# Conditioning vectors summed on VectorE, and three vectors broadcast through DRAM, in an adaLN + linear-attention + SwiGLU block

## The chip, the cores and the metric

The kernel runs on one core of a Trainium2 chip. Engines: PE (matmul), PEld (its weight load), DVE (VectorE), ACT (ScalarE), POOL (GpSimd), SP (the engine whose queue issues every DMA here). The metric is device time in microseconds (us), median of several executions. "Span" is first to last instruction; it is about 2 us less than the time. Each execution also reports the mean granted clock of PE: 1.000 is full speed.

## The reference, cut

```python
mod = silu(c) @ w_mod                  # [1,1024] @ [1024, 6*1024]
sa, ca, ga, sb, cb, gb = split(mod)    # six vectors of 1024
h = layernorm(x) * (1 + ca) + sa       # x: 2048 x 1024
x = x + ga * linear_attention(h)       # q, k -> phi = elu+1;  kv = sum k v;  z = sum k
h = layernorm(x) * (1 + cb) + sb
x = x + gb * ((silu(h @ w_gate) * (h @ w_up)) @ w_down)
```

All inputs are bf16. `ga` and `gb` multiply along the free dimension, so every partition needs the whole row ("broadcast"). `sb` and `1+cb` multiply along partitions, so one column per 128 features is enough. `z` is needed in both forms: as columns for the denominators, as a row for the matrix G.

## The kernel before

PE works through: chunk 0 (rows 0 to 511: Q, then K), chunks 1 to 3 (16 groups of eight 128x128x512 matmuls, 8 K and 8 Q), 16 G groups (16 matmuls each), the `wo` stage (16 row tiles), then four chunks of gate/up and down. The kernel's own helper finds the dependencies between engines from the tiles and hands PSUM banks over whole (a reader on another engine holds the bank). The late vectors ga, sb, cb and gb were made thus:

```python
def mod_col_mm(piece, kt):            # 8 per piece, 4 pieces: 256 matmuls of one column
    for m in range(NDT):
        P.pe("matmul", out=PS[:, 6, c0+m:c0+m+1], lhsT=STG[:, kt, m*128:(m+1)*128],
             rhs=SILUC[:, kt:kt+1], ...)
def mod_bcast(dst):                   # row form: columns repeated 128 times, times identity
    for nh in range(2):
        for d4 in range(4):
            P.pe("matmul", out=PS[:, bank, d4*128:(d4+1)*128], lhsT=MODREP[:, 4*nh+d4, :], rhs=IDENT[:], ...)
        P.act("activation", out=dst[:, nh*512:(nh+1)*512], in_=PS[:, bank, :], func=ACT.Copy)
# ... cut: chunks
def phi_evac(bank, dst):              # behind each Q or K group
    P.act(Exp  -> E1);  P.act(Relu -> RL)                 # shortened
    P.dve(min(E1,1)+1e-6 -> E1);  P.dve(RL + E1 -> dst)   # shortened
def th_mod(ch, dt):                   # scale and shift of the transposed h, chunks 2 and 3, all on ACT
    P.act("activation", out=HT[:, buf, dt, :], in_=HT[:, buf, dt, :], func=ACT.Identity, scale=..., bias=...)
# ... cut: after chunk 3
P.dma("wo", WO[:], wov)
# z: column copy, hi/lo split, ZSEL, then ZREP (columns repeated), all on DVE
z_bcast()                             # 16 PE matmuls ZREP x identity, two ACT copies -> ZB
g_group(0); g_evac(0); den()          # den: denominators, reciprocal, DRAM round trip -> RB
for g in range(1, 16):
    g_group(g); g_evac(g)             # 4 PSUM banks
    if g == 2: mod_bcast(GB_B)
```

Of the kernel before, what the change touches and what calls it, by code (L numbers as in the profile page):

```python
# [264 lines left out]
def bass_adaLN_cond__linear_attn_block__swiglu_ffn__prompt_kernel(  # L265
# [22 lines left out]
    with ExitStack() as es:  # L288
# [55 lines left out]
        RL = T("rl", 187 * KB, [128, 3, 512], BF16)  # L344
        MODREP = T("modrep", 190 * KB, [128, NDT, 128], BF16)
        GTMP = T("gtmp", 184 * KB, [128, 2, 512], FP32)
        KVT = T("kvt", 188 * KB, [128, NHG, 128], BF16)
        ZSEL = T("zsel", 193 * KB, [128, 288], BF16)
        ZREP = T("zrep", 194 * KB, [128, 2, NHG, 128], BF16)
        ZB = T("zb", 198 * KB, [128, D], FP32)  # L350
# [19 lines left out]
        RDR = nc.dram_tensor("recip_den", [32, S], BF16).ap()  # L370
        PSB = PS.bitcast(BF16)

        xv = A_x[0].rearrange("(t p) d -> p t d", p=128)
# [46 lines left out]
        P.act("activation", out=SILUC[:], in_=PSB[:, 1, 0:NDT], func=ACT.Silu)  # L420
        P.act("activation", out=ACTWARM[:], in_=SILUC[:], func=ACT.Exp)

        def ln1_stats_ops(st):
# [53 lines left out]
        def th_mod(ch, dt):  # L477
            buf = ch % 2
            P.act("activation", out=HT[:, buf, dt, :], in_=HT[:, buf, dt, :], func=ACT.Identity,
                  scale=MODCOL[:, 0, dt:dt + 1], bias=MODCOL[:, 1, dt:dt + 1])  # L480

# [77 lines left out]
        def phi_evac(bank, dst):  # L559
            i = phi_ctr[0] % 3  # L560
            phi_ctr[0] += 1
            P.act("activation", out=E1[:, i, :], in_=PS[:, bank, :], func=ACT.Exp)
            P.act("activation", out=RL[:, i, :], in_=PS[:, bank, :], func=ACT.Relu)
            P.dve("tensor_scalar", out=E1[:, i, :], in0=E1[:, i, :], scalar1=1.0, scalar2=1e-6,
                  op0=ALU.min, op1=ALU.add)
            P.dve("tensor_tensor", out=dst, in0=RL[:, i, :], in1=E1[:, i, :], op=ALU.add)
# [30 lines left out]

        def mod_col_mm(piece, kt):
            c0 = 8 * piece
            for m in range(NDT):  # L600
                P.pe("matmul", out=PS[:, 6, c0 + m:c0 + m + 1], lhsT=STG[:, kt, m * 128:(m + 1) * 128],
                     rhs=SILUC[:, kt:kt + 1], start=mcol_first[0], stop=(kt == NDT - 1), skip_group_check=True)
                mcol_first[0] = False

# [5 lines left out]

        def mod_col_fin(piece, idx, plus_one, bcast):
            c0 = 8 * piece
            P.dve("tensor_copy", out=MODTMP[:, 0:8], in_=PS[:, 6, c0:c0 + 8])
            if plus_one:
                P.dve("tensor_scalar", out=MODTMP[:, 0:8], in0=MODTMP[:, 0:8], scalar1=1.0, scalar2=None,
                      op0=ALU.add)
            if not bcast:
                P.dve("tensor_copy", out=MODCOL[:, idx, :], in_=MODTMP[:, 0:8])
            else:
                P.dve("tensor_copy", out=MODREP[:], in_=MODTMP[:, 0:8].unsqueeze(2).to_broadcast([128, NDT, 128]))  # L620

        def mod_bcast(dst):
            for nh in range(2):
                bank = [0, 7][nh]
                for d4 in range(4):
                    P.pe("matmul", out=PS[:, bank, d4 * 128:(d4 + 1) * 128], lhsT=MODREP[:, 4 * nh + d4, :],
                         rhs=IDENT[:], start=True, stop=True)
                P.act("activation", out=dst[:, nh * 512:(nh + 1) * 512], in_=PS[:, bank, :], func=ACT.Copy)

        def stg_load(piece):  # L630
            P.dma("stg%d" % piece, STG[:], wmv[:, :, 2048 + 1024 * piece:3072 + 1024 * piece])

# [61 lines left out]

        def piece_mm(side, piece, g0):
            for kt in range(NDT):
                add(side, g0 + kt, lambda kt=kt: mod_col_mm(piece, kt))

        s1, s2, s3 = {}, {}, {}
# [18 lines left out]
        for i, f in enumerate(ops):  # L718
            add(s1, 8 + (i * 7) // 12, f)
        piece_mm(s1, 0, 0)  # L720
        add(s1, 8, lambda: mod_col_fin(0, None, False, True))
        add(s1, 8, lambda: stg_load(1))
        add(s1, 13, lambda: mod_bcast(GA_B))
        add(s1, 15, lambda: ln1_rstd(3))
# [3 lines left out]
        for dt in range(NDT):  # L728
            add(s2, 7 + dt, lambda dt=dt: th_mod(3, dt))
        piece_mm(s2, 1, 0)  # L730
        add(s2, 8, lambda: mod_col_fin(1, 3, False, False))
        add(s2, 8, lambda: stg_load(2))
        piece_mm(s3, 2, 0)
        add(s3, 8, lambda: mod_col_fin(2, 2, True, False))
        add(s3, 8, lambda: stg_load(3))
        for kt in range(NDT):
            add(s3, 14 + kt // 4, lambda kt=kt: mod_col_mm(3, kt))
        chunk(1, s1)
        chunk(2, s2)
        chunk(3, s3)  # L740

        P.dma("wo", WO[:], wov)
        P.dve("tensor_copy", out=ZCOL[:], in_=PS[:, 6, 32:40])
        P.dve("tensor_copy", out=ZHL[:, 0, :], in_=ZCOL[:])
# [3 lines left out]
              in1=MASK4[:].unsqueeze(1).to_broadcast([128, NHG, 4]), op=ALU.mult)  # L748
        for i in range(2):
            P.dve("tensor_copy", out=ZREP[:, i, :, :], in_=ZHL[:, i, :].unsqueeze(2).to_broadcast([128, NHG, 128]))  # L750
        mod_col_fin(3, None, False, True)

        G_BANKS = [2, 3, 4, 5]

        def g_group(g):
            h, dt = g // NDT, g % NDT
            bank = G_BANKS[g % 4]
            for st in range(NST):
                P.pe("matmul", out=PS[:, bank, :], lhsT=XRES[:, st, dt * 128:(dt + 1) * 128],
                     rhs=PKH[h][:, st, :], start=(st == 0), stop=(st == NST - 1))  # L760

        def g_evac(g):
            h, dt = g // NDT, g % NDT
            bank = G_BANKS[g % 4]
            i = g % 2
            P.act("activation", out=GTMP[:, i, :], in_=ZB[:, h * 512:(h + 1) * 512], func=ACT.Copy,
                  scale=MODCOL[:, 1, dt:dt + 1])
            P.dve("scalar_tensor_tensor", out=G[:, dt, h * 512:(h + 1) * 512], in0=PS[:, bank, :],
                  scalar=MODCOL[:, 0, dt:dt + 1], in1=GTMP[:, i, :], op0=ALU.mult, op1=ALU.add)

        def z_bcast():
            for h in range(2):
                for hl in range(4):
                    for i in range(2):
                        P.pe("matmul", out=PS[:, h, hl * 128:(hl + 1) * 128], lhsT=ZREP[:, i, 4 * h + hl, :],
                             rhs=IDENT[:], start=(hl == 0 and i == 0), stop=(i == 1), skip_group_check=True)
                P.act("activation", out=ZB[:, h * 512:(h + 1) * 512], in_=PS[:, h, :], func=ACT.Copy)

        def den():
# [10 lines left out]
            P.wait_for("sp", wr)  # L790
            for hh in range(4):
                src = RDR.rearrange("(g x) s -> x g s", x=4)[hh].unsqueeze(0).to_broadcast([32, NHG, S])
                P.dma("rb%d" % hh, RB[32 * hh:32 * hh + 32, :, :], src)

# [31 lines left out]

        WO_BANKS = [0, 1, 2, 3]

# [11 lines left out]

        z_bcast()
        g_group(0)
        g_evac(0)
        den()
        for g in range(1, 16):
            g_group(g)
            g_evac(g)
            if g == 2:
                mod_bcast(GB_B)
            if 3 <= g <= 6:  # L850
                fold_ga(2 * g - 6)
                fold_ga(2 * g - 5)
            if g == 9:
                kvt_mm(0)
            if 11 <= g <= 14:
                m_mm(g - 11, [0, 1, 7])
            if 8 <= g <= 15:
                scale_pq(g - 8)
        for st in range(4):
# [4 lines left out]
        wo_part(1, 0, range(4))  # L864
        m_mm(4, [4, 5, 7])
        m_mm(5, [4, 5, 7])
        wo_part(1, 1, range(4))
        m_mm(6, [4, 5, 7])
# [40 lines left out]
        for st in range(NST):  # L909
# [3 lines left out]
            if st >= 1:  # L913
                ln2_sq(st - 1)
            if st == 6:
                for jj in range(4):
                    ln2_xn(jj)
# [4 lines left out]
        ln2_sq(NST - 1)  # L922

        y_ctr = [0]
        out_ops = []
        for ch in range(NCH):
            nxt = ch + 1 if ch + 1 < NCH else None
            for ft in range(NFT):
                q = 14 * ch + ft // 2
                slot = q % 4  # L930
                ftl = ft % 2
                gbank, ubank = (ft % 2) * 2, (ft % 2) * 2 + 1
                for dt in range(NDT):
# [9 lines left out]
                if ch == 0 and ft % 2 == 0 and ft < 14:  # L943
                    i = ft // 2
                    wt = WD_A[:, 4 * i:4 * i + 4, :] if i < 4 else WD_B[:, 4 * i - 16:4 * i - 12, :]
                    P.dma("wd%d" % i, wt, wdv[:, 4 * i:4 * i + 4, :])
                if nxt is not None and 4 <= ft < 8:
                    ln2_xn(4 * nxt + (ft - 4))
# [60 lines left out]
```

## Time and profile before

| | before |
|---|---|
| time, first three executions | 860.86 us median (860.63 to 862.51) |
| span of the profiled execution | 856.0 us |
| PE busy | 834.7 us (98%) |
| DVE, ACT busy | 257.8 us (30%), 219.9 us (26%) |

The page's first lines, and its row of the granted clock in 40 equal slices (9 means 90% or more):

```profile
span 856.0 us, 10690 instructions
...
PE 834.7 (98%) x4461; PEld 390.3 (46%) x4461; DVE 257.8 (30%) x563; ACT 219.9 (26%) x375; POOL 35.3 (4%) x50
...
PEclk9999999999999999999999999999999999999999
```

PE, busy for 98% of the span, is the limit. So a change helps if it removes PE work, or if it removes PE idle time. The view of PE's waits lists the idle time by what ended it (total us, times, longest):

```profile
PE ps L178 <- DMA wmsc<-in_w_mod_dram: 8.9, 3, 7.9
PE ps L178 <- ACT ht L178: 2.8, 4, 1.8
PE ps L178 <- DVE zrep L178: 2.5, 2, 2.1
PE ps L178 <- DVE xres L178: 1.9, 4, 1.0
PE ps L178 <- ACT mw L178: 0.5, 2, 0.3
```

The first line is the initial weight load, which the change does not touch. The line for ht holds the border between chunks 1 and 2, the line for zrep the border between chunk 3 and G. PE's timeline around these two borders (start, us, what, and in brackets the idle time in front and its releaser):

```profile
84.91 1.67 PE L178 MATMUL ps<-wqk,ht 128*128 128x512 bf16 x7
88.39 0.39 PE L178 MATMUL ps<-wqk,ht 128*128 128x512 bf16 x1 [1.81 <-ACT ht L178]
88.62 0.34 PE L178 MATMUL ps<-siluc,stg 128*128 128x1 bf16 x8
...
147.74 0.94 PE L178 MATMUL ps<-siluc,stg 128*128 128x1 bf16 x32
150.79 0.23 PE L178 MATMUL ps<-ident,zrep 128*128 128x128 bf16 x1 [2.11 <-DVE zrep L178]
151.40 1.01 PE L178 MATMUL ps<-ident,zrep 128*128 128x128 bf16 x15 [0.37 <-DVE zrep L178]
152.24 3.62 PE L178 MATMUL ps<-pk_85,xres 128*128 128x512 bf16 x16
```

At 88.39 PE waits 1.81 us for the last scaled ht tile; the last of the eight matmuls of chunk 2's first group needs it. Eight one-column matmuls on stg, as at 88.62, take 0.20 us up to the next start. Between the stg matmuls of 147.74 and the first G matmul at 152.24 lie 0.8 us for those matmuls, 2.5 us of idle time in two parts and the 16 zrep matmuls. ACT's timeline shows why ht is late at the first border (start, us, ..., how many):

```profile
84.16 1.53 ACT L178 ACTIVATE ht<-ht,modcol 128x512 bf16<-128x512 bf16 x2
85.57 1.10 ACT L178 ACTIVATE ga_b<-ps 128x512 bf16<-128x512 f32 x2
86.52 0.63 ACT L178 ACTIVATE e_90<-ps 128x512 bf16<-128x512 f32 x1
...
87.48 0.86 ACT L178 ACTIVATE ht<-ht,modcol 128x512 bf16<-128x512 bf16 x1
```

ACT has no gap here: ht scalings, the two copies of the broadcast ga (1.10 us), Exp and Relu follow each other, and the ht tile of 87.48 is the one PE waits for.

### The profile page before, as it was taken

The numbers are of one execution on the slowest core, as the hardware profiler recorded it, in microseconds if no ns is written. First come the engines' busy times: TensorE is split into PE (matmuls) and PEld (weight loads), VectorE is DVE, ScalarE is ACT, GpSimd is POOL, SyncE is SP. The second block draws the span as 40 slices with busy tenths as digits, with TensorE's granted clock in tenths as the row PEclk, the third lists the DMA queues.
The fourth block names the chain that finished last, engine by engine and source line by source line (L and its number), as shares of the span: only waits on it lengthen the run. The fifth ranks groups of instructions, "written<-read, shape, count | busy, mean of one in ns | idle before, by whom it ended". The sixth has DMA issues, their size and how long they took to land.

```text
span 856.0 us, 10690 instructions
## 1 busy us (share of the span) xinstructions
PE 834.7 (98%) x4461; PEld 390.3 (46%) x4461; DVE 257.8 (30%) x563; ACT 219.9 (26%) x375; POOL 35.3 (4%) x50
## 2 busy tenths in 40 slices
PE   4989999999999999999999999999999999999998
PEld 3444444444444444444444444444444444444444
DVE  4667443537554221211122111122111112112111
ACT  4667775212334111110111111011111101111101
POOL 1000000000021000020000003000000200000000
PEclk9999999999999999999999999999999999999999
DMA  9925313461456896560155554025555303553000
GB/s 305 376 107 148 93 57 105 149 148 36 160 124 172 255 306 176 148 154 25 36 159 157 156 150 111 25 62 148 152 159 159 90 25 105 148 148 99 0 25 25
DMA packets 169616, 110.93 MB, mean 130 GB/s; under 512 B 28128, under 2 KB 154208, under 8 KB 169568
## 3 DMA queue, kind: packets, MB, share of 16 engines
q1 hardware_dynamic: 169568, 110.25, 45.1%
q8 instruction: 35, 0.57, 0.3%
q14 instruction: 13, 0.11, 0.0%
HBM read 99.62 MB, written 4.33 MB: 121 GB/s over the span
## 4 chain that ended last, share of the span: by engine, by line
PE 93%; ACT 2%; DMA 2%; SPq 1%; DVE 1%; issue 0%; ACTq 0%
PE ps L178 93%; DMA wmsc<-in_w_mod_dram 2%; SPq L178 1%; ACT ht L178 1%; ACT rl L178 1%; ACT e_90 L178 1%; DMA ht<-xres 0%; DVE zrep L178 0%; ACT mw L178 0%; DVE xres L178 0%; ACT ga_b L178 0%; DVE pqt L178 0%; DVE stats L178 0%; DVE pk_85 L178 0%; DVE zhl L178 0%
## 5 line engine op out<-in xcount | busy, mean ns | idle before, releaser
L178 DVE TENSOR_TENSOR at<-sg,ps 128x512 bf16<-128x512 bf16 x112 | 77.1, 688 | 299.9 <-PE ps L178 298.3
L178 ACT ACTIVATE sg<-ps 128x512 bf16<-128x512 f32 x112 | 66.9, 597 | 310.5 <-PE ps L178 310.5
L178 PE MATMUL ps<-wd_a,at 128*128 128x512 bf16 (+2 forms) x528 | 115.9, 373 | 0.0
L178 PE MATMUL ps<-wd_b,at 128*128 128x512 bf16 (+2 forms) x396 | 88.3, 373 | 0.0
L178 PEld LDWEIGHTS ps<-wd_a,at 128*128 128x128 bf16 x528 | 51.1, 98 | 59.8
L178 ACT ACTIVATE att<-ps 128x512 bf16<-128x512 f32 (+1 forms) x32 | 19.0, 594 | 179.7 <-PE ps L178 179.7
L178 DVE TENSOR_TENSOR ut<-att,gb_b 128x512 bf16<-128x512 bf16 (+1 forms) x32 | 14.3, 447 | 165.1 <-ACT att L178 165.1
L178 PE MATMUL ps<-wqk,ht 128*128 128x512 bf16 x256 | 60.3, 379 | 2.5 <-ACT ht L178 2.5
L178 PE MATMUL ps<-ht,wqk 128*128 128x512 bf16 x256 | 59.2, 386 | 0.3 <-ACT ht L178 0.3
L178 PEld LDWEIGHTS ps<-wd_b,at 128*128 128x128 bf16 x396 | 38.3, 98 | 44.7
L178 PE MATMUL ps<-mw,pqt 128*128 128x512 bf16 x256 | 55.9, 379 | 0.0
L178 PE MATMUL ps<-h2t,guu_108 128*128 128x512 bf16 x224 | 52.9, 379 | 0.0
L178 PE MATMUL ps<-h2t,guu_109 128*128 128x512 bf16 x224 | 52.9, 379 | 0.0
L178 PE MATMUL ps<-h2t,gug_106 128*128 128x512 bf16 x224 | 52.9, 379 | 0.0
L178 PE MATMUL ps<-h2t,gug_103 128*128 128x512 bf16 x224 | 52.9, 379 | 0.0
L178 PE MATMUL ps<-h2t,guu_107 128*128 128x512 bf16 x224 | 52.9, 379 | 0.0
L178 PE MATMUL ps<-h2t,gug_104 128*128 128x512 bf16 x224 | 52.9, 379 | 0.0
L178 PE MATMUL ps<-h2t,gug_105 128*128 128x512 bf16 x224 | 52.9, 379 | 0.0
L178 PE MATMUL ps<-h2t,guu_110 128*128 128x512 bf16 x224 | 52.9, 379 | 0.0
L178 ACT ACTIVATE e_90<-ps 128x512 bf16<-128x512 f32 x64 | 38.7, 604 | 34.5 <-PE ps L178 30.7
L178 POOL TENSOR_SCALAR h2t<-h2t,modcol 128x512 bf16<-128x512 bf16 x32 | 25.2, 808 | 393.6 <-DMA h2t<-xn_111 393.6
L178 PEld LDWEIGHTS ps<-mw,pqt 128*128 128x128 bf16 x256 | 25.0, 98 | 29.7
(108 smaller groups left out, 676.0 us busy)
## 6 DMA issues: line engine op xcount, KB each, us to landing
stg<-in_w_mod_dram SPq DMA_DIRECT2D x4, 2048.0 KB, 8.7
gug_103<-in_B_w_gate_dram SPq DMA_DIRECT2D x14, 512.0 KB, 4.2
guu_107<-in_B_w_up_dram SPq DMA_DIRECT2D x14, 512.0 KB, 5.4
gug_104<-in_B_w_gate_dram SPq DMA_DIRECT2D x14, 512.0 KB, 4.0
guu_108<-in_B_w_up_dram SPq DMA_DIRECT2D x14, 512.0 KB, 5.3
gug_105<-in_B_w_gate_dram SPq DMA_DIRECT2D x14, 512.0 KB, 4.0
guu_109<-in_B_w_up_dram SPq DMA_DIRECT2D x14, 512.0 KB, 5.3
gug_106<-in_B_w_gate_dram SPq DMA_DIRECT2D x14, 512.0 KB, 4.0
```

Source lines behind the costliest of these rows:

```text
L178: return getattr(e, method)(**kw)
```

## The change

The intent: take the late vectors off PE. DVE has idle time (30% busy), so it sums `silu(c)[k] * w_mod[k, :]` in fp32 into a 128x1024 accumulator, splits it into high and low bf16 parts, and PE only adds the 128 partitions up (16 one-column matmuls per vector instead of 64). The rows ga, gb and z are written to DRAM and read back with a broadcast access, instead of PE matmuls and ACT copies. G groups start at once behind chunk 3, with five banks, and z and den are worked out behind them. To make room, half of the ht scalings go to DVE and each phi is finished one group later.

```diff
+        def macc(src, kt):                      # kt == 0: tensor_scalar mult (cut)
+                P.dve("scalar_tensor_tensor", out=ACC[:], in0=src[:, kt, :], scalar=SILUF[:, kt:kt + 1], in1=ACC[:],
+                      op0=ALU.mult, op1=ALU.add)
+        def macc_split():
+            P.dve("tensor_copy", out=MHL[:, 0, :], in_=ACC[:])
+            P.dve("tensor_tensor", out=MHL[:, 1, :], in0=ACC[:], in1=MHL[:, 0, :], op=ALU.subtract)
-        def mod_col_mm(piece, kt):              # 64 matmuls per vector (body cut)
+        def mod_cols(c0, first=None):
             for m in range(NDT):
+                for i in range(2):
+                    P.pe("matmul", out=PS[:, 6, c0 + m:c0 + m + 1], lhsT=MHL[:, i, m * 128:(m + 1) * 128],
+                         rhs=ONES[:, 0:1], start=mcol_first[0], stop=(i == 1), skip_group_check=True)
-        def mod_bcast(dst):                     # (body cut)
+        def mod_fin_row(c0, i, dst):            # ga, gb
+            P.dve("tensor_copy", out=MROW[:, i, :], in_=PS[:, 6, c0:c0 + 8])
+            wr = P.dma("mdw%d" % i, MDR[i].rearrange("(m p) -> p m", p=128), MROW[:, i, :], allow_slow_non_contiguous=True)
+            P.wait_for("sp", [wr])
+            P.dma("mdr%d" % i, dst[:], MDR[i].unsqueeze(0).to_broadcast([128, D]))
 ... phi_evac: E1 and RL on ACT as before; the two DVE operations now by phi_flush()
+            phi_pend.append((i, dst))
+            if len(phi_pend) > 1:
+                phi_flush()
 ... th_mod: even dt as P.dve("tensor_scalar", ...), odd dt on ACT
 ... chunk 2: macc of ga (groups 4-11), chunk 3: macc of cb; sb in wo tiles 1-4, gb in wo tiles 8-15
+        zw = P.dma("zw", ZDR[0].rearrange("(g p) -> p g", p=128), ZCOL[:], allow_slow_non_contiguous=True)
+        P.wait_for("sp", [zw])
+        P.dma("zr", ZB[:], ZDR[0:1, :].to_broadcast([128, D]))
         P.dma("wo", WO[:], wov)
-        z_bcast()                               # (body cut)
 ... G loop: five banks, evacuation 3 groups behind at first, den() behind group 1
 ... gate/up, chunk 0:
+                if ch == 0 and ft == 3:
+                    mod_cols(8)
+                    mod_fin_row(8, 1, GB_B)
```

The diff also holds smaller edits that are not shown: the read of rb in eight parts instead of four, other PSUM banks for G, `wo` and gate/up, one `wo` part split in two, and the first rows of the second LayerNorm one row tile later.

## The prediction

> **What bounds the kernel now.** The page: PE 834.7 us busy of an 856.0 us span, chain of waits 93% on PE. DVE and ACT are at 30% and 26%, the granted clock is 1.0 throughout. What shortens it is fewer PE cycles, or less of its 21 us idle. The view of waits lists PE's: 8.9 us for the first w_mod loads and 2.2 for c, 2.8 for ACT ht, 2.5 for DVE zrep, 1.9 for DVE xres, 0.5 for ACT mw.

> **PE work removed and added** (PE's timeline, start to start of the next group):
> - Eight one-column matmuls on stg take 0.20 us. All 256: -6.4 us.
> - Eight matmuls ident/modrep take 0.44 us, twice: -0.9 us. Sixteen on zrep: -0.9 us.
> - Added: 4 x 16 one-column matmuls at 0.025 us: +1.6 us.
> Net -6.6 us, nearly all on the critical path.

> **PE idle removed.**
> - zrep: PE idles 2.1+0.4 us between the last Q group and z_bcast. Afterwards G groups (3.45 us each, free banks) fill this: -2.5 us.
> - Chunk 1 to 2 (PE idle 1.8 us at 88.4): ACT is full from 77.7 to 88.4 with exp, relu, eight ht scalings (0.7 us apart) and two ga_b copies (1.1). Half the scalings go to DVE (0.41 us each) and ga_b goes to a DMA: -1.8 us.
> - Near 44 us PE waits for DVE xres. Deferring each phi by one group puts one phi (0.6 us) and some waits behind these: -0.5 to -1.
> - mw waits: -0.5.
> Sum about -5.5 us.

> **What moves to DVE and DMA.** 32 fp32 accumulations of 128x1024. No such form is in the trace; from the [...] 128x512 forms (0.69 to 0.75 us) I estimate 1.1 to 1.2 us each, about 36 us, plus four splits of about 1.9 us. [...] In chunks 2 and 3 DVE then needs about 1.9 us per group against PE's 1.8: a backlog of 1 to 2 us, which five banks and three E1 buffers absorb. Tightest is the wo stage, row tiles 1 to 4: two wo_res (0.78 each with the accumulator read) plus two accumulations make 3.8 us against PE's 3.46, then the split. The backlog may reach the four banks around tile 7: +0 to 1 us.
> The z row goes out as 1024 four-byte pieces and comes back broadcast. [...] no run here shows the time yet. I allow 10 us for the trip; five banks give PE about 19 us before group 5 needs group 0 evacuated. rb, which takes 27 us from issue in the trace, is needed no earlier than now.

> **Prediction.** 860.9 - 6.6 - 5.5 + 0.5 = about 849 us (-1.4%). Eight in ten: 845 to 853.5. Faster by over 2% (below 843.7) 0.06, within 2% 0.92, slower 0.02.

> **What would show it.** Page: PE busy near 828 us, about 4270 matmuls; DVE up by some 35 us. Waits: zrep gone, no PE idle at the chunk 1 to 2 border, nothing on zb. Timeline: accumulations of 1.1 us; chunk 3 running straight into G. The FFN's 585 us unchanged within 1 us.

> **What would make it wrong.** Element-wise DRAM writes far slower than 10 us, so G stalls on zb, or wo and rb come late behind it (one queue). Accumulations slower than 1.2 us, so that DVE starves PE in chunk 2 or the wo stage. The deferred phi holding E1 buffers so long that ACT, then PE, stalls.

What stands there without a trace: the 1.1 to 1.2 us per accumulation are the estimate from 128x512 forms of before's trace (xres<-ps,xres takes 0.69 us, g<-ps,modcol,gtmp 0.75), the 1.9 us of a split can be read as 0.69 (the 128x1024 copy zrep<-zhl) plus 1.2, and the 10 us for the trip through DRAM are an allowance that no trace gave.

## The result, and the profile after

The changed kernel takes 850.28 us median (849.45 to 853.83, 4 runs) against 860.75 us (4 runs): ratio 0.9885, 95% interval 0.9852 to 0.9918. A ratio here is the mean time of one kernel's fast runs over that of the other's of the same rounds, so it is not quite the ratio of the medians. A second set (below, after_again) gave 850.92 against 860.23 us, ratio 0.9889 [0.9868, 0.9910].

```profile
span 848.9 us, 10203 instructions
...
PE 824.1 (97%) x4157; PEld 384.2 (45%) x4237; DVE 298.5 (35%) x608; ACT 212.0 (25%) x361; POOL 39.2 (5%) x50
...
PEclk9999999999999999999999999999999999999999
```

PE's busy time fell by 10.6 us, DVE's rose by 40.7 us. Of PE's busy time not all is work taken away: 80 matmul records are missing from this trace (4157 matmuls, but 4237 weight loads). The stages below are therefore measured by start times.

PE's waits, to be read against the list of before:

```profile
PE ps L178 <- ACT xres L178: 8.6, 1, 8.6
PE ps L178 <- DMA guu_113<-in_B_w_up_dram: 2.6, 1, 2.6
PE ps L178 <- ACT ht L178: 1.9, 2, 1.0
PE ps L178 <- DVE xres L178: 1.4, 3, 1.0
PE ps L178 <- DMA wmsc<-in_w_mod_dram: 1.0, 3, 0.5
```

The waits for zrep and mw are gone or small, and ht is down by 0.9 us. The first line is the same initial idle time as wmsc in before (8.9 us there), put down to another releaser. One entry is new: 2.6 us for guu, a weight tile of the gate/up stage.

```profile
84.54 8.80 PE L178 MATMUL ps<-wqk,ht 128*128 128x512 bf16 x39
...
133.16 8.79 PE L178 MATMUL ps<-ht,wqk 128*128 128x512 bf16 x39
141.79 3.62 PE L178 MATMUL ps<-pk_85,xres 128*128 128x512 bf16 x16
145.24 0.54 PE L178 MATMUL ps<-ones,mhl 128*128 128x1 bf16 x16
...
302.99 1.89 PE L178 MATMUL ps<-h2t,guu_112 128*128 128x512 bf16 x8
307.47 1.90 PE L178 MATMUL ps<-h2t,gug_109 128*128 128x512 bf16 x8 [2.59 <-DMA guu_113<-in_B_w_up_dram]
```

The first group of chunk 2 (84.54) has no wait in front of it. Chunk 3 runs into G at 141.79 without idle time. Against before, chunk 2 to the end of chunk 3 (from the end of chunk 2's first group, 88.62 before and 84.54 + 1.73 = 86.27 after, to 148.54 and 141.79) takes 55.5 us instead of 59.9: 4.4 us less, which is 24 x 0.20 us of stg matmuls less 0.41 us for one set of 16 (145.24 to 145.65 shows such a set). At 152.24 against 141.79, G starts 10.5 us earlier. At the end only 7.1 us of span are left. 2.6 us went at 307.47, in front of gate/up tile 12; the queue of SP shows what happened (start, us in issuing, what):

```profile
278.54 1.21 SPq L178 DMA_DIRECT2D mod_row<-mrow  x1
295.43 0.34 SPq L178 DMA_DIRECT2D gb_b<-mod_row  x1
...
296.36 0.44 SPq L926 DMA_DIRECT2D gug_109<-in_B_w_gate_dram  x1
296.84 2.38 SPq L926 DMA_DIRECT2D guu_113<-in_B_w_up_dram  x1
```

The gb row's write is issued at 278.54. The next entry, the read, waits for it and goes out at 295.43, 16.9 us later. All weight loads stand behind this wait in program order: the load of slot 2 (gug_109, guu_113), whose buffer PE had done with at about 284.2, is issued at 296.4, and PE gets there first. The times to landing (KB, then us from issue; the two mod_row writes as a median):

```profile
zb<-z_row SPq DMA_DIRECT2D x1, 512.0 KB, 3.9
...
mod_row<-mrow SPq DMA_DIRECT2D x2, 2.0 KB, 15.0
...
z_row<-zcol SPq DMA_DIRECT2D x1, 4.0 KB, 10.6
```

The write of z (1024 pieces of 4 bytes) took 10.6 us and its read 3.9; G's five banks hid that. The two rows ga and gb (1024 pieces of 2 bytes) took 13.1 and 16.9 us, 15.0 in the median. DVE's accumulations (busy us in total, mean ns of one), with the split:

```profile
L178 DVE SCALAR_TENSOR_TENSOR acc<-stg,siluf,acc 128x1024 f32<-128x1024 bf16 x14 | 17.9, 1278 | 0.0
...
L178 DVE TENSOR_TENSOR mhl<-acc,mhl 128x1024 bf16<-128x1024 f32 x4 | 4.9, 1225 | 0.1
...
L178 DVE CAST mhl<-acc 128x1024 bf16<-128x1024 f32 x4 | 2.8, 691 | 0.1
```

One accumulation takes 1.28 us, a little more than the 1.1 to 1.2 estimated; a split takes 0.69 + 1.23 us.

**The clock.** The profiled execution of before had a clock of 1.000, that of after 0.998. In after's trace the clock record is 0.5 from 47.08 to 50.50 us; in the PEclk row, with 21 us to a slice, this does not show. This record lasts 3.413 us, and e10's view below has 0.50 over 3.41 us. Half of that is lost, so one window costs about 1.7 us: in e10, eight gate/up matmuls that lie in one take 3.36 us from start to start (273.81 to 277.17) instead of 1.73. This is not a property of the change: 33 executions of before in the experiments report 1.000 down to 0.994, 0 to 3 windows. So two numbers are given for each kernel below: the mean of span x clock, in which these windows are taken out, and the windows per execution, (1 - clock) x span / (0.5 x 3.413 us). The clock is reported to 0.001, half a window.

### The profile page after: what moved, and what is told of

It reads as the page before. It is cut to its first block, busy times and chain, and to the rows that moved or that the text cites. A ratio compares the mean times of both kernels' runs of the same rounds, so it can differ in the third digit from the quotient of the medians.

```text
span 848.9 us, 10203 instructions
## 1 busy us (share of the span) xinstructions
PE 824.1 (97%) x4157; PEld 384.2 (45%) x4237; DVE 298.5 (35%) x608; ACT 212.0 (25%) x361; POOL 39.2 (5%) x50
## 4 chain that ended last, share of the span: by engine, by line
PE 91%; DMA 3%; SPq 2%; DVE 2%; issue 1%; ACT 1%; POOL 0%; DVEq 0%; ACTq 0%
PE ps L178 91%; SPq L178 2%; DMA xres<-in_A_x_dram 2%; DMA guu_113<-in_B_w_up_dram 1%; DVE xres L178 0%; DVE stats L178 0%; DVE pqt L178 0%; DVE acc L178 0%; ACT ht L178 0%; ACT rl L178 0%; DVE mhl L178 0%; ACT e_90 L178 0%; POOL rstd L178 0%; DVE e_90 L178 0%; ACT mw L178 0%
## 5 line engine op out<-in xcount | busy, mean ns | idle before, releaser
L178 PE MATMUL ps<-wqk,ht 128*128 128x512 bf16 x247 | 58.2, 384 | 1.6 <-ACT ht L178 1.0
L178 POOL TENSOR_SCALAR h2t<-h2t,modcol 128x512 bf16<-128x512 bf16 x32 | 27.2, 865 | 397.1 <-DMA h2t<-xn_115 380.8
```

The costliest lines, as they stand in the source:

```text
L178: return getattr(e, method)(**kw)
```

## The experiments

| kernel | time, us median | ratio to before [95%] | span x clock, us | half-clock windows per run |
|---|---|---|---|---|
| before (three sets, 33 runs) | 861.2, 860.9, 860.2 | 1 | 855.7, 855.4, 855.7 | 1.7 |
| after (two sets, 9 runs) | 850.3, 850.9 | 0.9885, 0.9889 | 847.1, 846.9 | 1.2 |
| e1_gb_wait_late | 847.08 | 0.9836 [0.9811, 0.9862] | 844.1 | 0.7 |
| e2_gb_runs | 847.35 | 0.9841 [0.9816, 0.9866] | 844.7 | 0.6 |
| e3_no_defer | 853.92 | 0.9918 [0.9893, 0.9944] | 849.6 | 1.7 |
| e4_before_defer | 859.65 | 0.9983 [0.9959, 1.0007] | 854.8 | 1.7 |
| e5_mod_act | 847.44 | 0.9848 [0.9826, 0.9871] | 845.4 | 0.2 |
| e6_z_pe | 853.97 | 0.9922 [0.9902, 0.9942] | 849.6 | 1.5 |
| e7_no_gap44 | 843.85 | 0.9809 [0.9786, 0.9832] | 842.0 | 0.2 |
| e8_ga_cb_pe | 850.07 | 0.9880 [0.9858, 0.9901] | 847.4 | 0.6 |
| e9_gaps_short | 862.74 | 1.0029 [1.0008, 1.0050] | 859.8 | 0.7 |
| e10_gaps_long | 895.12 | 1.0401 [1.0377, 1.0425] | 882.9 | 6.0 |

All eleven gave correct results (after_again is the row "after", second set). e1 to e4, e5 to e8, and the last three ran on three chips, each with its own runs of before; those agree within 0.4 us in span x clock, so the column may be compared across sets to about that.

### e1_gb_wait_late: is it the queue's wait?

```diff
+            def fetch():                       # for gb; ga as before
+                P.wait_for("sp", [wr])
+                P.dma("mdr%d" % i, dst[:], MDR[i].unsqueeze(0).to_broadcast([128, D]))
 ... gate/up, chunk 0
+                if ch == 0 and ft == 9:
+                    gb_fetch[0]()
```

> After, but the queue's wait for the gb row's write and the broadcast read come at gate/up tile 9 instead of directly behind the write at tile 3; the write itself stays. Theory (the queue is held by that wait, so the load of weight slot 2 goes out 13 us late): the PE wait of 2.6 us on guu at 305 us goes, the span falls by about 2.6 us, time about 847.5. Rival (the 1024 two-byte pieces themselves, or other traffic, fill the DMA engines): the load goes out early but lands late, the PE wait stays at 1 to 3 us, time about 850.

Time 847.08 us; the guu wait is gone and PE runs through gate/up tile 12. Span x clock fell by 2.9 us from after's 847.0. The queue of SP in e1:

```profile
277.20 1.07 SPq L178 DMA_DIRECT2D mod_row<-mrow  x1
...
283.04 0.37 SPq L934 DMA_DIRECT2D gug<-in_B_w_gate_dram  x1
283.45 0.58 SPq L934 DMA_DIRECT2D guu<-in_B_w_up_dram  x1
284.08 14.30 SPq L178 DMA_DIRECT2D wd_a<-in_B_w_down_dram  x1
```

The write still goes out at 277.20, but the load of slot 2 now leaves at 283.04 and 283.45 and is in time. The theory holds. The rival has a share: the next load behind it takes 14.3 us to issue (284.08; the same load in e2, where the row is written in 8 runs, takes 4.7), so the rows' small pieces do hold up the queue even without the wait; here nothing needs it that early.

### e2_gb_runs: is it the number of pieces?

```diff
+            if i == 1:
+                P.pe("transpose", out=PSB[0:NDT, 7, 0:128], in_=MROW[:, i, :], identity=IDENT[:])
+                P.dve("tensor_copy", out=CS8[0:NDT, :], in_=PSB[0:NDT, 7, 0:128])
+                wr = P.dma("mdw1", MDR[1].rearrange("(m p) -> m p", p=128), CS8[0:NDT, :])
```

> After, wait in place, but the gb row is transposed on PE (one small transpose) and written as 8 runs of 256 bytes instead of 1024 pieces of 2 bytes. Theory (the landing time comes from the number of pieces): the write lands in 2 to 4 us instead of 16.9, the PE wait on guu goes, time about 847.5. Rival (the write lands late because of the 2 MB of weight loads issued just before it on the same queue): landing stays over 10 us and so does the PE wait, time about 850.

```profile
278.51 0.83 SPq L178 DMA_DIRECT2D mod_row<-cs  x1
283.11 0.35 SPq L178 DMA_DIRECT2D gb_b<-mod_row  x1
...
285.14 0.38 SPq L931 DMA_DIRECT2D gug<-in_B_w_gate_dram  x1
```

The read follows the write after 4.6 us instead of 16.9, and the load of slot 2 leaves at 285.14. Time 847.35 us, no guu wait. I expected a landing of 2 to 4 us and got a little more, beside the same weight loads. So most of the 16.9 us are those of the 1024 two-byte pieces. The queue in front has a smaller share: in after the first piece of the gb row starts at 281.98, 3.4 us after its issue, and in e2 the first run starts 3.6 us after its issue; for the ga row, with no weight load just in front, it is 0.9 us. The price is 0.5 us of PE idle time in front of the small transpose.

### e3_no_defer and e4_before_defer: what is the deferred phi worth?

e3 is after with the deferral undone, e4 is before with the deferral alone:

```diff
-            if len(phi_pend) > 1:        # e3
-                phi_flush()
+            phi_flush()
```

> After, but each phi is finished at once as before, not one group later. If deferring is what the kernel's gain in chunks 1 to 3 rests on, DVE then stands behind ACT in front of each accumulation and PE gets new waits there: time 851 to 853. If it is worth nothing (my prediction had it at 0.5 to 1 us near 44 us, and the profile of after shows no gain there): 850 within 0.5. The dip of the granted clock at 47 us (0.5 for 3.4 us, costing about 1.7 us): if deferring causes it, the mean clock returns to 1.000 and time falls to about 848.5; if not, it stays at 0.998.

> Before, with the deferred phi alone. My prediction had it worth 0.5 to 1 us (PE's wait for xres near 44 us, 1.9 us in all): time about 860.0. By the profile of after, this wait is the same length with it (1.7 us), because DVE works through the same statistics first: 860.8 within 0.5. If deferring causes the dip of the clock, the mean clock is 0.998 here and time is 1 to 2 us above before.

e4: span x clock 0.8 us below that of before, ratio interval containing 1. Its PE waits for xres near 45 us are 1.4 us (before: 1.9), and the wait at the border of chunks 1 and 2 is 1.17 us (before: 1.81; first line below). So alone it gives at most a microsecond. e3 took 853.92 us, above the 851 to 853 that I expected, and costs 2.6 us of span x clock against after. Part of it is the second line, from its PE timeline:

```profile
88.48 0.39 PE L178 MATMUL ps<-wqk,ht 128*128 128x512 bf16 x1 [1.17 <-ACT ht L178]
...
125.37 0.35 PE L178 MATMUL ps<-ones,pk 128*128 128x1 bf16 x8 [1.24 <-DVE mrow L178]
```

In e3 PE waits 1.24 us because DVE, standing behind ACT in front of each phi, comes late to the copy of the ga column, and that copy holds PSUM bank 6, which PE's next z matmuls need. In after this wait does not exist. So deferring pays in chunk 3, where DVE is full; a gain near 44 us, where I had put it, is not shown (see the end). The rest of the 2.6 us is not settled: the guu wait is 3.7 us in e3's trace, but in after's two traces it is itself 2.6 and 4.3 us. Both kernels have half-clock windows (1.7 per run), so the deferral neither makes nor removes them.

### e5_mod_act: the split of the ht scalings

e1 with `th_mod` on ACT alone, as in the kernel before.

> e1 (after with the gb wait moved; 847.1 us) with all ht scalings of chunks 2 and 3 on ACT again. Theory: the 1.8 us that PE waited between chunks 1 and 2 in before came from ACT being full; without the ga_b copies (1.1 us) part of it is left: PE waits 0.7 to 1.5 us for ACT ht at the border of chunks 1 and 2, time 847.8 to 848.6. Rival: removing the ga_b copies and deferring phi was enough, no wait appears there, time within 0.5 of e1.

```profile
86.36 7.30 PE L178 MATMUL ps<-wqk,ht 128*128 128x512 bf16 x33 [1.13 <-ACT ht L178]
```

The wait at the border is back at 1.13 us; span x clock rises by 1.3 us. So of the 1.8 us in before, about two thirds needed the split. The rest is what the deferral alone did in e4 (1.81 to 1.17), so that nearly nothing is left for the two ga_b copies that I had counted on; this rests on one trace of each. The median time, 847.44 us, is below the 847.8 to 848.6 that I expected: these four runs had fewer half-clock windows (0.2 per run) than e1.

### e6_z_pe: z through DRAM, behind the G groups

e1 with the 16 zrep matmuls and two ACT copies in front of the G groups again; `zw`, the wait and `zr` are removed.

> e1 with z broadcast by PE before the G groups, as before, instead of through DRAM behind them. Theory: PE waits about 2.5 us for DVE zrep again and does 0.9 us of matmuls, and the DVE split of cb (1.9 us) now stands in front of zrep, so that the wait may be longer: span times granted clock up by 3.4 to 5 us. The new gap also costs clock: more half-clock windows of 3.4 us (1.7 us each) than e1's 0.7 per run. Time 851 to 853. Rival (G could not really start earlier, and other waits absorb it): under 1.5 us more.

```profile
143.40 0.23 PE L178 MATMUL ps<-ident,zrep 128*128 128x128 bf16 x1 [2.88 <-DVE zrep L178]
144.01 1.53 PE L178 MATMUL ps<-ident,zrep 128*128 128x128 bf16 x15 [0.38 <-DVE zrep L178]
```

The waits for zrep are 2.88 us plus 0.38; span x clock is up 5.5 us and the time is 853.97 us, both a little over what I expected, and windows are up from 0.7 to 1.5 per run. Part of this is dearer than before's zrep: here DVE's split of cb (138.62 to 140.57) stands in front of it. This is the largest part of the change's gain that is idle time, and the runs show that nothing else absorbs it.

### e8_ga_cb_pe: the sums on DVE

e1 with ga and cb (two of four vectors) summed by one-column matmuls on PE:

```diff
-            add(s2, 4 + kt, lambda kt=kt: macc(STG, kt))
-        add(s2, 13, macc_split)
+            add(s2, 4 + kt, lambda kt=kt: mm_pe(0, kt))      # 8 matmuls on STG; cb likewise in s3
```

> e1 with ga and cb summed by 128 one-column matmuls on PE again instead of 16 accumulations and two splits on DVE. By 0.025 us each, 128 matmuls against the 32 that read the DVE sums are 96 x 0.025 = 2.4 us more PE work, all on the critical path: span times granted clock up 2.4, time 849.5. Rival (PE has hidden slack in chunks 2 and 3, because it waits for ACT or DVE there anyway): less than 1 us more.

Span x clock is up by 3.3 us (2.4 expected; its five runs spread from 845.3 to 849.3). The one-column matmuls had no slack to hide in: the rival, under 1 us, is out.

### e9_gaps_short and e10_gaps_long: what the half-clock windows come from

In the traces, windows often begin where a PE gap ends: 150.3 us in e4 (zrep), 144.3 in e6 (zrep), 308.5 in e3 and 306.5 in after_again (guu). To test it, e1 got 16 more PE waits in the gate/up tiles, with one or three DVE copies in each:

```diff
+                if ft % 7 == 2:
+                    for _ in range(3):          # 1 in e9
+                        P.dve("tensor_copy", out=GAP[:], in_=PS[:, ubank, :])
+                    P.pe("matmul", out=PS[:, 7, 0:1], lhsT=GAP[:, 0:128], rhs=ONES[:, 0:1], start=True, stop=True)
```

> e1 with 16 extra PE waits in the gate/up tiles, each behind one DVE copy of a 128x512 PSUM bank (about 0.9 us of PE idle). Wrong on purpose in no output; only time is added. Theory (half-clock windows come from PE gaps, and the longer the gap the likelier): gaps of 0.9 us give few windows: 0.7 to 2 per run; span times clock up by 16 x 0.9 to 1.1 = 14 to 18 us. Rival (windows come by chance, at a rate per time): 0.7 per run as in e1, here and in the long gaps.

> The same with three copies in each of the 16 waits (about 2.2 us of PE idle, the length of the zrep wait in before and of the guu wait in after). Theory: windows per run rise well above e1's 0.7, to 4 to 12, so that each gap costs clearly more than its length; span times clock up by 35 to 40 us. Rival (chance[...]): about 0.7 windows per run, and time rises by the gaps alone.

> The changed kernel unaltered, for more executions of it on the chip of the two gap runs, with before beside it. Expected: 850 within 1, about 1.2 half-clock windows per run, span times granted clock about 847, 8.5 below that of before.

after_again came out as expected (850.92 us, 1.2 windows, 846.9). The 16 gaps of 0.79 us gave 0.7 windows per run, as many as e1 without them. The 16 gaps of 2.24 us gave 6.0 (5 to 7). So the rival, chance, does not fit. e10's windows table, for the stretch of two gaps and for 3.41 us behind each (us, busy of PE, PEld, DVE, ACT, POOL with counts, granted clock, DMA share, GB/s):

```profile
271.52:273.76 2.24, 0.01 (x1) 0.00 (x1) 2.13 (x4) 0.00 (x0) 0.00 (x0) 1.00 1.16 313
273.74:277.15 3.41, 3.39 (x9) 1.21 (x10) 0.56 (x1) 0.00 (x0) 0.00 (x0) 0.50 0.65 238
300.18:302.42 2.24, 0.00 (x2) 0.01 (x1) 2.13 (x4) 0.00 (x0) 0.00 (x0) 1.00 0.53 132
302.42:305.83 3.41, 3.36 (x16) 1.60 (x18) 0.54 (x1) 0.60 (x1) 0.00 (x0) 1.00 0.99 267
```

### e7_no_gap44: a version faster than both

```diff
-            add(kside, 4 + r, lambda r=r: th_round(1, r, 7 if r % 2 == 0 else 6, "act"))
+            add(kside, min(5 + r, 7), lambda r=r: th_round(1, r, 7 if r % 2 == 0 else 6, "act" if r % 2 == 0 else "dve"))
-            if 1 <= st <= 4:             # sb: two accumulations per row tile, split at tile 4
+            for kt in {1: [0, 1], 2: [2], 3: [3, 4], 4: [5], 5: [6, 7]}.get(st, []):
```

> e1 with two edits: chunk 1's transposes one K group later and half of their evacuations on DVE (against the PE gaps at 44 to 46 us and at 54 to 57 us, together about 2 us), and sb's accumulations spread over row tiles 1 to 5 of the wo stage (against a backlog of 0.3 us). Expected: span times granted clock down by 1.5 to 2.5 us. If the half-clock windows come from PE gaps, windows per run also fall, from 0.7 to about 0.3. Time 844 to 845.5.

843.85 us, ratio 0.9809 to before: 1.9% faster than before, and its interval does not meet those of after. Span x clock is 2.1 us below e1, and PE's waits for xres and ht come to 0.8 us in all. The two edits were not tried apart. One of five runs had a window. It is the best version.

## Why the prediction was right, point by point

The time (849 predicted, 850.3 measured, range 845 to 853.5) and the class (within 2%) were right. With the one wait removed that was not in the sum, e1's span x clock is 11.5 us below that of before in the same rounds (855.67 - 844.14), and the sum said 11.6 (6.6 + 5.5 - 0.5). That they agree so closely is in part luck: not all terms of the sum were right, as the list shows.

- **PE work, -6.6 us: right.** Chunks 2 and 3 lost 4.4 us, which is what 0.20 us per eight matmuls gives for them. e8 put half of the vectors back and lost 3.3 us.
- **zrep, -2.5 us idle and -0.9 us work: right.** 4.5 us between the last stg matmuls' start and G became none of idle; e6 undid it and lost 5.5 us, windows not counted.
- **Chunk border, -1.8 us: right in size.** No wait there in after; e5 brings back 1.13 us. The split and the deferral did it; a part of the ga_b copies is not shown (e4, e5).
- **"Near 44 us ... -0.5 to -1": not shown.** PE's idle time from 43 to 57 us was 2.6 us before (0.48 + 0.23 + 0.96 + 0.23 + 0.39 + 0.28) and is 2.6 us after (0.23 + 0.96 + 0.23 + 0.22 + 0.97): what was gained on xres came back as a wait for ht. But one pair of traces does not decide it. In the eight other traces that run the same code in this stage (after_again, e1, e2, e5, e6, e8, e9, e10) it is 0.95 to 2.75 us, and in e3, without the deferral, 1.85. The worth of the deferral that is seen lies in chunk 3 (e3) and at the border of chunks 1 and 2 (e4).
- **mw, -0.5 us: 0.3.** One wait of 0.16 us remains.
- **DVE backlog in the wo stage, 0 to +1 us: about +0.3.** PE's adding-up matmuls start at 231.12, when the split ends, and the next row tile at 231.79 instead of 231.53.
- **Trip through DRAM, 10 us allowed: 14.5 for z.** It was within the 19 us of slack that I had read from the five banks (five of the 16 G groups that take 61.2 us), so it cost nothing.
- **Left out of the sum: the gb row's trip, +2.6 us (2.6 and 4.3 in two traces).** I had named "late behind it (one queue)" as a risk for wo and rb, but I never asked who stands behind gb's wait: the weight loads. I priced the trip for the row that is needed soon, z, and took the row needed late as free. Its own consumer had time; the queue's other users had not.
- **"The FFN's 585 us unchanged within 1 us": wrong.** From the first gate/up matmul to the end of the span it is 582.9 us before and 586.0 after. Of the 3.1 us, 2.6 are the wait above and 0.4 the adding up of gb, which now lies in this stage; in e1, without the wait, it is 583.3.
- **"The granted clock is 1.0 throughout": true of one profile, not of the kernel.** Before loses 1.7 windows of about 1.7 us per run on average, after 1.2. The three sets of before alone lie between 1.4 and 2.0, so it is not shown that the change altered this number.

Two things stay open. Windows also begin behind cells with less idle time than in e10: at 45.7 to 47.1 us in three traces (after, e2, e5; PE busy for 1.84 to 1.88 us, that is at most 1.6 us idle), at 21.3 to 25.3 us in four (e1, e3, e6, e8; 1.3 to 1.7 us idle, beside waits for the first w_mod loads), and at 150.34 in e4 (1.6 us idle), while in before a cell with 1.7 us idle at 149.4 has none behind it. So idle time alone does not sort these cases. Part of the busy time in such cells is small transposes and one-column matmuls, but no run here shows how those count. And the times in which the 1024 small pieces are finally written are not in the trace: their packets all begin within 5 us of the issue, the landing follows 9 us (z) to 12 us (gb) later.

## What to carry to other kernels

The wait for gb's write in the queue of SP (16.9 us) was paid by the weight load behind it (2.6 us of PE idle time), not by the data it waits for: put the issue and the wait far apart (e1, no such idle time left), or make the first transfer short by writing long runs (e2, 4.6 us instead of 16.9). Moving work to an engine with idle time paid in full here (3.3 us for two vectors, e8), because the busy engine was the limit, as long as each new order (bank handovers above all, 1.24 us in e3) still let that engine run ahead. And of 16 PE gaps of 2.24 us, six led to a window and so cost about 1.7 us more than their length (e10), while 16 of 0.79 us added no windows (e9), so close the long ones first. Last, keep several traces of one kernel before you read a gain of half a microsecond from one stage: near 44 us the same code idled between 0.95 and 2.75 us.
